# Two units of lead, second weights counted into it, and raw heads loaded in pairs: an attention and two MoEs on one core

## The chip, the core and the metric

One core of a Trainium2 chip runs one program: an attention of 4 batches, 8 heads, 576 positions and 64 dimensions a head, and two MoE layers over its 2304 tokens. The metric is the device time of one execution in microseconds (us); the median of three is 1420.57 (1418.37 to 1425.62). In this text PE is TensorE, DVE is VectorE, ACT is ScalarE, POOL is GpSimd and SP is SyncE, whose queue issues all transfers here.

## What is computed

The reference, cut to what matters (`B, H, S, D = 4, 8, 576, 64`):

```python
scores = (q @ k.T) / sqrt(D) + bias[h]          # bias[h][i, j]: a small MLP of log1p(|i - j|) / log1p(max(i, 1))
attn = exp(scores - max(scores)); attn /= sum(attn) + 1e-9
x = (attn @ v).transpose(0, 2, 1, 3).reshape(2304, 512)
g = x @ w_gate                                   # 512 x 1536
x = (g * sigmoid(g) * (x @ w_val)) @ w_out       # 1536 x 512
h = maximum(x @ w_in, 0)                         # 512 x 2048
out = (h * h) @ w_out2                           # 2048 x 512
```

The weights come as 64-bit floats, which are decoded on the chip. Each large product is made of three products of 16-bit halves.

## The kernel before, in words

**Work.** The attention is 144 *items*: ten phases (lines 52 and 938) of 4 or 8 heads, two batches a head. Phases 0 to 3, and the "m" among them, make batches 0 and 1, phases 5 to 9 batches 2 and 3. For an item, PE multiplies `qT` and `kT` (line 809), DVE adds the bias and finds the maximum (818), ACT takes the exponential (824), ACT or POOL casts it to 16 bits (833, 830), POOL makes the rest (222), SP issues the transpose of both halves into `pT` (852, three buffers of `pt` and of `pT`), and PE multiplies `pT` by the values (874). A phase over, `finish_unit` writes the normalised rows of one *unit* of 256 tokens to `x_d`, and `done[0]` says that MoE unit may start.

**First MoE.** Nine units (`moe1`, line 423): twelve steps of 24 matmuls (459), whose gate ACT and DVE make (`th`, lines 467 to 470), then POOL the low half of `z` (222), and 72 matmuls of `w_out` (481). A step's product stands in one of three PSUM banks. Around it run the decoding of the first weights (`w_stream`) and the bias (`bias_all`), whose matmuls are line 643.

**Second MoE.** `weights2` (line 1191) loads the second weights in 32 pieces of 512 KB into `w2s`, three rooms, decodes each on DVE (lines 258 to 263), scales them, and combines them in eight parts (`combine`, line 1164, on DVE, ACT and POOL). Then five chunks follow, each with a hidden part (1329) and an output part (1361).

**Order.** Python generators yield after each piece of work, and a loop at line 1275 takes the next step of the attention's side (`a_all`) or of the MoE's side (`m_all`). The MoE's side steps when `at[0]`, the items begun, has reached what `LEAD` gives for the work done so far in the MoE (`pos["m"]`; a unit counts 46.8):

```python
lead = w_done[0] >= 0 and at[0] >= float(np.interp(pos["m"], *LEAD))
if m_ok and (lead or not a_ok):
```

A scheduler then orders each engine's instructions; every engine, and SP's queue, takes its own in that order.

**Late heads.** Values and keys of batches 2 and 3 take the place of those of batches 0 and 1. Each head of one batch is loaded alone by `load_head` (line 675): a first part of 512 positions, and the last 64 positions twice, to both halves of the partitions, three transfers in all. `feed` (line 1072) calls it: values for their norm (`norm_v`) at items 32 to 47; keys from item 55 on, with `split_k` at items 56 to 71; values again at 58 to 73, with `split_v` an item later. The keys have two buffers (`late["k"]`), and so have the second values (`vr[:, 16]` and `late["v"]`, which lies in `wr`).

Of the kernel before, what the change touches and what calls it, by code (L numbers as in the profile page):

```python
# [10 lines left out]
F32 = mybir.dt.float32  # L11
F16 = mybir.dt.float16
# [9 lines left out]
B, H, S, D = 4, 8, 576, 64  # L22
DM, FF1, FF2 = 512, 1536, 2048
NT = B * S
P = 128
# [9 lines left out]
}  # L35

LEAD = [0, 47, 94, 140, 187, 234, 281], [16, 35, 53, 72, 97, 121, 144]
SQK = 16.0

CZ = 2.0 ** -48  # L40
# [36 lines left out]
def tile_attention_moe(  # L77
# [4 lines left out]
    nc = tc.nc  # L82
# [21 lines left out]
    st = {}  # L104
# [111 lines left out]
    def mixed(k):  # L216

        mix_n[k] = mix_n.get(k, -1) + 1
        return MIX[k][mix_n[k] % len(MIX[k])]
# [452 lines left out]
            nc.sync.dma_start(  # L672
                f[64 * e:64 * e + 64, :, 256:320], v[b, hs, 512:S, :].rearrange("h p d -> p h d"))

    def load_head(dst, src, n, b):

        nc.sync.dma_start(dst[:, 0:256], src[b, n, 0:512, :].rearrange("(p r) d -> p (r d)", r=4))
        for e in range(2):
            nc.sync.dma_start(dst[64 * e:64 * e + 64, 256:320], src[b, n, 512:S, :])

    def norm_v(bp, i, raw):
        nc.scalar.activation(junk1[:, 0:320], raw, AF.Square, accum_out=vss[bp][:, i:i + 1])
# [24 lines left out]
        st["sv", bp] = keep(16)  # L707
        nc.vector.tensor_copy(st["sv", bp], pb[:, 0:16])

    def split_v(bp, i, raw):  # L710

        o = vh[:, i, :].rearrange("p (c w) -> p c w", c=5)
        halves(o[:, :, 64:128], o[:, :, 0:64], raw.rearrange("p (c d) -> p c d", d=D),
               st["sv", bp][:, i:i + 1], mixed("V"))

    def split_k(i, raw):

# [295 lines left out]
    at = [0]  # L1013
# [30 lines left out]
    vr = att.tile([P, 17, 5 * D], F32, name="vr", bufs=1)  # L1044
# [16 lines left out]
    late = {}  # L1061

    def open_late():

        pre_stack.close()
        pool = a_stack.enter_context(tc.tile_pool(name="late", bufs=1, side="right"))
        lt = pool.tile([P, 960], F32, name="late")
        late["k"] = [lt[:, 320 * i:320 * i + 320] for i in range(2)]
        late["ks"] = lt[:, 640:960].bitcast(F16)
        late["v"] = wr.t[:, 36, 0:320]  # L1070

    def feed(idx, after):

        if not after:
            return
        if idx < 16:
            if idx in (1, 3):
                prep_k(2 + idx // 2)
            if 2 <= idx < 10:
                for i in (2 * idx - 4, 2 * idx - 3):  # L1080
                    norm_v(0, i, vr[:, i + 1, :])
            if idx == 12:
                scale_v(0, ma)
            if idx == 15:
                for j in range(6):
                    nc.gpsimd.memset(ptw[:, j // 2, 640 * (j % 2) + S:640 * (j % 2) + 640], 0.0)
        elif idx < 32:
            i = idx - 16
            split_v(0, i, vr[:, i + 1, :])
        elif idx < 48:  # L1090
            i = idx - 32
            if i:
                norm_v(1, i - 1, late["v"])
            load_head(late["v"], v, i // 2, 2 + i % 2)
        elif idx == 48:
            norm_v(1, 15, late["v"])
            scale_v(1, ma)

        i = idx - 56
        if -1 <= i < 15:  # L1100
            j = i + 1
            load_head(late["k"][j % 2], k, j // 2, 2 + j % 2)
        if 0 <= i < 16:
            split_k(i, late["k"][i % 2])
        if 2 <= i < 18:
            j = i - 2
            load_head((vr[:, 16, :], late["v"])[j % 2], v, j // 2, 2 + j % 2)
        if 3 <= i < 19:
            split_v(1, i - 3, (vr[:, 16, :], late["v"])[(i - 3) % 2])

    def start():
        load_k(0)
# [122 lines left out]
    def a_all():  # L1235
        yield from start()
        yield from merge((attend(), 25.5), (w_stream(), 70.0), (bias_all(), 29.0))
        yield from named(weights2(), "w")

    def m_all():  # L1240
        for m in range(9):
# [199 lines left out]
```

## Time and profile before

| what | value |
|---|---|
| median of three runs | 1420.57 us |
| the profiled execution | 1426.94 us |
| its span, first to last instruction | 1425.1 us |
| PE busy | 1159.7 us (81%) |
| DVE, ACT, POOL busy | 865.1, 662.5, 709.2 us |
| granted TensorE clock, mean | 0.904 |
| moved by DMA | 163.59 MB |

Busy is the time in which an engine worked on anything. An engine's share of the whole span says little here, since the stages have different limits: the first 199 us hold the first weights and the first phase, 199 to 830 the rest of the attention, and from 1140 on the chunks of the second MoE run alone. The granted clock is the share of full speed that the throttle let TensorE have.

### The profile page before, as it was taken

How to read it: one execution, taken by the hardware profiler on the slowest of the kernel's cores; microseconds unless marked ns; L12 is line 12 of the kernel's file. 1: busy time of each engine (PE TensorE's matmuls, PEld its weight loads, DVE VectorE, ACT ScalarE, POOL GpSimd, SP SyncE). 2: the span in 40 equal slices, each digit the busy share in tenths (PEclk: the TensorE clock that was granted, in tenths of full speed). 3: DMA queues.
4: the chain of work that ended last, by engine and by line, in shares of the span. 5: the costliest groups of instructions: out<-in, count | busy, mean ns of one | idle time of the engine just before them, and what ended most of it. 6: DMA issues, size and time to landing. Idle time of an engine off the chain costs nothing. (4 is left out here: it accounts for less than half of the span.)

```text
span 1425.1 us, 28069 instructions
## 1 busy us (share of the span) xinstructions
PE 1159.7 (81%) x10620; PEld 846.5 (59%) x10620; DVE 865.1 (61%) x1944; ACT 662.5 (46%) x1492; POOL 709.2 (50%) x766
## 2 busy tenths in 40 slices
PE   2459847988969943798998999958376899999998
PEld 2348736757648622575867676746133667667587
DVE  5997999854563543545446432248878666472925
ACT  5555676666654654445545532224452242332322
POOL 2763678667764522445555521103188844362713
PEclk9999868988978965699999999979687999999999
DMA  9776568577684667969899940065600102010000
GB/s 233 174 184 167 130 162 170 100 152 147 132 167 91 137 150 148 196 117 208 156 198 195 170 82 16 9 171 184 199 1 0 30 31 45 16 30 30 15 31 16
DMA packets 359507, 163.59 MB, mean 115 GB/s; under 512 B 323404, under 2 KB 334412, under 8 KB 359372
## 3 DMA queue, kind: packets, MB, share of 16 engines
q1 hardware_dynamic: 359372, 161.80, 51.5%
q8 instruction: 83, 1.36, 0.4%
q14 instruction: 52, 0.43, 0.1%
HBM read 76.94 MB, written 25.03 MB: 72 GB/s over the span
## 5 line engine op out<-in xcount | busy, mean ns | idle before, releaser
L459 PE MATMUL mm<-xT,wr 128*128 128x256 f16 x2592 | 310.4, 278 | 23.2 <-DMA xT<-x_d 15.4
L459 PEld LDWEIGHTS <-wr 128*128 128x128 f16 x2592 | 253.5, 100 | 61.1 <-issue 24.9
L1151 POOL TENSOR_TENSOR x<-x 128x256 f32<-128x256 f32 (+1 forms) x160 | 154.1, 972 | 150.2 <-ACT x L1338 145.2
L222 POOL TENSOR_TENSOR pt<-s,pt 128x576 f16<-128x576 f32 x128 | 167.2, 1311 | 91.9 <-ACT pt L833 81.5
L1329 PE MATMUL mm<-wr,w2r 128*128 128x512 f16 (+1 forms) x960 | 195.9, 366 | 0.0
L222 POOL TENSOR_TENSOR z<-th,z 128x256 f16<-128x256 f32 x108 | 78.8, 730 | 181.1 <-ACT z L442 171.6
L874 PE MATMUL av<-vr,pT 128*128 128x64 f16 (+3 forms) x2160 | 110.5, 208 | 54.3 <-DMA pT<-pt 41.1
L1329 PEld LDWEIGHTS <-w2r 128*128 128x128 f16 x960 | 95.5, 100 | 95.2 <-issue 8.5
L481 PE MATMUL mm<-wr,z 128*128 128x512 f16 x648 | 148.7, 379 | 0.0
L818 DVE CUSTOM_DVE_ANT_0 s<-qk,bh 128x576 f32<-128x576 f32 x144 | 107.8, 751 | 61.2 <-PE qk L809 32.0
L824 ACT ACTIVATE s<-s,sc 128x576 f32<-128x576 f32 x144 | 111.0, 771 | 67.8 <-DVE sc L823 51.5
L874 PEld LDWEIGHTS <-pT 128*128 128x128 f16 (+3 forms) x2160 | 90.0, 110 | 80.7 <-DMA pT<-pt 51.1
L618 POOL TENSOR_TENSOR btmp<-btmp,xs 128x256 f32<-128x256 f32 (+1 forms) x108 | 88.3, 820 | 97.6 <-ACT btmp L617 68.5
L1361 PEld LDWEIGHTS <-wr 128*128 128x128 f16 x1134 | 111.8, 99 | 31.5 <-DVE wr L1151 7.7
L809 PE MATMUL qk<-kT,qT 128*128 128x288 f16 x512 | 102.9, 339 | 16.6 <-DVE sc L818 9.9
L599 DVE TENSOR_TENSOR mask<-tabT,theta 128x1024 f16<-128x1024 f16 (+1 forms) x108 | 85.7, 809 | 34.2 <-PE ma L643 33.4
L468 DVE SCALAR_TENSOR_TENSOR th<-th,mm 128x256 f32<-128x256 f32 x108 | 45.0, 417 | 99.8 <-ACT th L467 99.6
L481 PEld LDWEIGHTS <-z 128*128 128x128 f16 x648 | 61.0, 98 | 67.0 <-issue 1.1
L1334 ACT ACTIVATE x<-mm 128x512 f32<-128x512 f32 (+1 forms) x80 | 43.6, 553 | 116.0 <-DVE wr L1151 57.0
L643 PEld LDWEIGHTS <-mask 128*128 128x128 f16 x1440 | 68.4, 113 | 46.5 <-DVE mask L599 23.4
L830 POOL TENSOR_SCALAR pt<-s 128x576 f16<-128x576 f32 x64 | 44.8, 700 | 86.4 <-ACT s L824 44.7
L624 POOL TENSOR_TENSOR bst<-bst,btmp 128x256 f32<-128x256 f32 (+1 forms) x108 | 83.6, 777 | 6.7 <-POOL btmp L618 0.5
(241 smaller groups left out, 2003.7 us busy)
## 6 DMA issues: line engine op xcount, KB each, us to landing
bh<-bias_d SPq DMA_DIRECT2D x64, 288.0 KB, 3.3
bias_d<-bst SPq DMA_DIRECT2D x36, 256.0 KB, 3.1
w2s<-in_moe_w_in_dram SPq DMA_DIRECT2D x16, 512.0 KB, 4.5
w2s<-in_moe_w_out_dram SPq DMA_DIRECT2D x16, 512.0 KB, 4.3
wr<-in_moe_w_gate_dram SPq DMA_DIRECT2D x24, 256.0 KB, 5.4
wr<-in_moe_w_val_dram SPq DMA_DIRECT2D x24, 256.0 KB, 4.7
wr<-in_moe_w_out_dram SPq DMA_DIRECT2D x9, 512.0 KB, 3.7
y_d<-yh SPq DMA_DIRECT2D x18, 256.0 KB, 2.6
```

Source lines behind the costliest of these rows:

```text
L222: nc.gpsimd.tensor_tensor(out=out_, in0=x, in1=hi, op=ALU.subtract)
L459: nc.tensor.matmul(pg[:, 256 * gi:256 * gi + 256], wr.parts(key, f // 4, cc, wl, P * (f % 4), P), mov(xl, cc), start=k == 0, stop=k == 11)
L481: nc.tensor.matmul(po, zall[:, f, zl, P * t:P * t + P], wr.parts("o", 0, f, wl), start=k == 0, stop=k == 3 * NF1 - 1)
L599: nc.vector.tensor_tensor(out=m[:, :, ni * e:ni * e + ni], in0=block(kb, i0, ni), in1=th, op=ALU.is_gt)
L618: nc.gpsimd.tensor_tensor(out=tmp[r], in0=tmp[r], in1=xb, op=ALU.mult)
L809: nc.tensor.matmul(pq[:, j, 0:288], qT[:, j0 + s, :], kT[:, 2 * n + i, js], start=s == 0, stop=s == 1)
L818: nc.vector.tensor_tensor_reduce(out=s.rearrange("p (a j) -> p a j", a=2), in0=pq[:, :, 0:288], in1=bias.rearrange("p (a j) -> p a j", a=2 ...
L824: nc.scalar.activation(s, s, AF.Exp, bias=nm, scale=-1.0, accum_out=total)
L874: nc.tensor.matmul(av[r, slot, 0:64], pT[:m, a, r], vh[:m, k0, o:o + 64], start=j == 0, stop=j == len(terms) - 1)
L1151: (nc.gpsimd if how else nc.vector).tensor_tensor(out=out_, in0=a, in1=b, op=op)
L1329: nc.tensor.matmul(ph[:, :n], w2r.parts("w", g // 4, cc, wl, P * (g % 4), P), yt[:, 4 * yl + cc, :], start=m == 0, stop=m == 11)
L1361: nc.tensor.matmul(po, HS[f][:, o:o + P], st["C7"][f][wl][:, b:b + 256], start=f == 0 and k == 0, stop=f == 7 and k == 2)
```

## The change

Three things change.

1. `LEAD` has new numbers. Unit 0 waits for item 32 (16 before), unit 1 for about 60, unit 2 for 88, unit 3 for 116, unit 4 for 144.
2. `at[0]` goes on to grow with the steps of `weights2`, which count 86.6 in all, so from unit 4 on the MoE's steps alternate with those of the second weights.
3. `load_head` gives way to `load_two`: a head of two batches at a time, one transfer for the first part and one for the tail, which goes to the lower 64 partitions only. It is called at every second item, and at the next both heads of the pair are normed or split. Keys and the first values share one buffer of two heads, `late["k"]`, whose upper half of the tail is cleared once by POOL; the second values have one pair in `late["v"]` and `late["vt"]`, and `split_v` makes two pieces of such a head, so ACT and DVE each have 16 instructions more, on 64 rows.

```diff
-LEAD = [0, 47, 94, 140, 187, 234, 281], [16, 35, 53, 72, 97, 121, 144]
+LEAD = [0, 47, 94, 141, 188, 330, 420], [32, 60, 88, 116, 144, 226, 232]
...
-    def load_head(dst, src, n, b):
-
-        nc.sync.dma_start(dst[:, 0:256], src[b, n, 0:512, :].rearrange("(p r) d -> p (r d)", r=4))
-        for e in range(2):
-            nc.sync.dma_start(dst[64 * e:64 * e + 64, 256:320], src[b, n, 512:S, :])
+    def load_two(main, tail, src, n, bp):
+
+        bs = slice(2 * bp, 2 * bp + 2)
+        nc.sync.dma_start(main, src[bs, n, 0:512, :].rearrange("b (p r) d -> p b (r d)", r=4))
+        nc.sync.dma_start(tail, src[bs, n, 512:S, :].rearrange("b p d -> p b d"))
...
-    def split_v(bp, i, raw):
+    def split_v(bp, i, raws_):
 
         o = vh[:, i, :].rearrange("p (c w) -> p c w", c=5)
-        halves(o[:, :, 64:128], o[:, :, 0:64], raw.rearrange("p (c d) -> p c d", d=D),
-               st["sv", bp][:, i:i + 1], mixed("V"))
+        c0 = 0
+        for raw in raws_:
+            m, n = raw.shape[0], raw.shape[1] // D
+            halves(o[:m, c0:c0 + n, 64:128], o[:m, c0:c0 + n, 0:64], raw.rearrange("p (c d) -> p c d", d=D),
+                   st["sv", bp][:m, i:i + 1], mixed("V"))
+            c0 += n
...
-        lt = pool.tile([P, 960], F32, name="late")
-        late["k"] = [lt[:, 320 * i:320 * i + 320] for i in range(2)]
-        late["ks"] = lt[:, 640:960].bitcast(F16)
-        late["v"] = wr.t[:, 36, 0:320]
+        lt = pool.tile([P, 1152], F32, name="late")
+        late["k"] = lt[:, 0:640].rearrange("p (b x) -> p b x", b=2)
+        nc.gpsimd.memset(late["k"][64:P, :, 256:320], 0.0)
+        late["ks"] = wr.t[:, 36, 0:320].bitcast(F16)
+        late["v"] = lt[:, 640:1152].rearrange("p (b x) -> p b x", b=2)
+        late["vt"] = wr.t[0:64, 36, 320:448].rearrange("p (b x) -> p b x", b=2)
...
         i = idx - 56
-        if -1 <= i < 15:
-            j = i + 1
-            load_head(late["k"][j % 2], k, j // 2, 2 + j % 2)
         if 0 <= i < 16:
-            split_k(i, late["k"][i % 2])
-        if 2 <= i < 18:
-            j = i - 2
-            load_head((vr[:, 16, :], late["v"])[j % 2], v, j // 2, 2 + j % 2)
+            if i % 2 == 0:
+                load_two(late["k"][:, :, 0:256], late["k"][0:64, :, 256:320], k, i // 2, 1)
+            else:
+                for j in range(2):
+                    split_k(i - 1 + j, late["k"][:, j, :])
         if 3 <= i < 19:
-            split_v(1, i - 3, (vr[:, 16, :], late["v"])[(i - 3) % 2])
+            if i % 2:
+                load_two(late["v"], late["vt"], v, (i - 3) // 2, 1)
+            else:
+                for j in range(2):
+                    split_v(1, i - 4 + j, [late["v"][:, j, :], late["vt"][:, j, :]])
...
-        yield from named(weights2(), "w")
+        for c in named(weights2(), "w"):
+            if not isinstance(c, tuple):
+                at[0] += c
+            yield c
```

The values for the norm, at items 32 to 47, change in the same way as the keys.

SP's queue while the late keys and values come in, before (`late` is a key buffer, `vr` and `wr` are value buffers, `pT` the transposed probabilities, `bh` a bias):

```order
L677 DMA late<-in_k_dram 128x256
L679 DMA late<-in_k_dram 64x64 x2
L677 DMA wr<-in_v_dram 128x256
L679 DMA wr<-in_v_dram 64x64 x2
L789 DMA bh<-bias_d_66 128x576
L852 DMA_TRANSPOSE pT<-pt 128x10x128
L677 DMA late<-in_k_dram 128x256
L679 DMA late<-in_k_dram 64x64 x2
L677 DMA vr<-in_v_dram 128x256
L679 DMA vr<-in_v_dram 64x64 x2
L852 DMA_TRANSPOSE pT<-pt 128x10x128
```

The same place now, where line numbers from 680 on are four higher (`late<-in_v_dram` is the first part of a pair of values, `wr<-in_v_dram` its tail):

```order
L856 DMA_TRANSPOSE pT<-pt 128x10x128 x2
L678 DMA late<-in_k_dram 128x2x256
L679 DMA late<-in_k_dram 64x2x64
L678 DMA late<-in_v_dram 128x2x256
L679 DMA wr<-in_v_dram 64x2x64
L793 DMA bh<-bias_d_66 128x576
L856 DMA_TRANSPOSE pT<-pt 128x10x128 x2
L678 DMA late<-in_v_dram 128x2x256
L679 DMA wr<-in_v_dram 64x2x64
L678 DMA late<-in_k_dram 128x2x256
L679 DMA late<-in_k_dram 64x2x64
```

Between two transposes stood the six transfers of one key head and one value head; now four transfers, of a pair of each, stand between two transposes and the next two.

DVE's queue where the decoding of the second weights begins, before (`xh` are the rows of unit 8, `w2r<-w2s` a decoding step, `th` the gate, here of unit 8, the last one):

```order
L921 SCALAR_TENSOR_TENSOR xh<-bh,ux,xh 128x256 x2
L921 SCALAR_TENSOR_TENSOR xh<-x_11859,ux,xh 128x256 x2
L258 TENSOR_SCALAR w2r<-w2s 128x512
L261 SCALAR_TENSOR_TENSOR w2r<-w2s,w2r 128x512
L263 SCALAR_TENSOR_TENSOR w2r<-w2s,w2r 128x512
L258 TENSOR_SCALAR w2r<-w2s 128x512
L261 SCALAR_TENSOR_TENSOR w2r<-w2s,w2r 128x512
L258 TENSOR_SCALAR w2r<-w2s 128x512
L263 SCALAR_TENSOR_TENSOR w2r<-w2s,w2r 128x512
L468 SCALAR_TENSOR_TENSOR th<-th,mm 128x256
L261 SCALAR_TENSOR_TENSOR w2r<-w2s,w2r 128x512
L470 SCALAR_TENSOR_TENSOR th<-th,mm 128x256
```

And now, where the gates are those of unit 4, with unit 5 behind it:

```order
L468 SCALAR_TENSOR_TENSOR th<-th,ma 128x256
L468 SCALAR_TENSOR_TENSOR th<-th,mm 128x256
L470 SCALAR_TENSOR_TENSOR th<-th,ma 128x256
L468 SCALAR_TENSOR_TENSOR th<-th,mm 128x256
L470 SCALAR_TENSOR_TENSOR th<-th,mm 128x256 x2
L258 TENSOR_SCALAR w2r<-w2s 128x512
L261 SCALAR_TENSOR_TENSOR w2r<-w2s,w2r 128x512
L263 SCALAR_TENSOR_TENSOR w2r<-w2s,w2r 128x512
L258 TENSOR_SCALAR w2r<-w2s 128x512
L468 SCALAR_TENSOR_TENSOR th<-th,ma 128x256
L261 SCALAR_TENSOR_TENSOR w2r<-w2s,w2r 128x512
L470 SCALAR_TENSOR_TENSOR th<-th,ma 128x256
```

The decoding stood after unit 7 and among the steps of unit 8; it now stands after the sixth step of unit 4 and among the steps of units 4 and 5, and most of the combination stands in units 6 and 7, the rest in unit 8, instead of after unit 8.

## Rows read from the trace of the kernel before

**Rows 1.** The page, part 1: engine, busy us (share of the span), instructions.

```profile
PE 1159.7 (81%) x10620; PEld 846.5 (59%) x10620; DVE 865.1 (61%) x1944; ACT 662.5 (46%) x1492; POOL 709.2 (50%) x766
```

**Rows 2.** Windows: stretch, length, busy us (instructions) of engines, granted clock, DMA.

```profile
199.00:494.00 295.00, 253.15 (x2932) 193.86 (x2931) 186.99 (x472) 179.89 (x445) 196.52 (x247) 0.87 0.68 138
494.00:588.00 94.00, 45.10 (x417) 29.91 (x415) 40.84 (x129) 45.23 (x94) 29.60 (x27) 0.59 0.74 159
588.00:830.00 242.00, 228.38 (x2430) 169.61 (x2429) 124.96 (x450) 127.05 (x289) 126.34 (x132) 0.97 0.92 174
635.00:670.00 35.00, 30.86 (x276) 18.64 (x275) 21.25 (x85) 21.46 (x48) 18.36 (x17) 0.91 1.02 203
830.00:930.00 100.00, 95.91 (x790) 69.98 (x787) 26.16 (x75) 27.40 (x65) 16.03 (x24) 1.00 0.10 23
930.00:1033.00 103.00, 57.84 (x439) 41.34 (x439) 77.57 (x199) 38.87 (x86) 18.33 (x19) 0.78 0.64 192
1033.00:1140.00 107.00, 83.29 (x444) 45.94 (x445) 83.22 (x93) 36.94 (x71) 90.22 (x78) 0.84 0.05 10
```

**Rows 3.** Windows of line 824 alone (exponential and its accumulator, two records an item).

```profile
494.00:588.00 94.00, 15.48 (x36) 0.59 0.74 159
635.00:670.00 35.00, 11.56 (x27) 0.91 1.02 203
```

**Rows 4.** Timeline of SP, 546 to 556: start us, us, engine, line, transfer, count.

```profile
546.11 1.33 SPq L852 DMA_TRANSPOSE pT<-pt  x1
547.48 0.70 SPq L677 DMA_DIRECT2D late<-in_k_dram  x1
548.58 1.13 SPq L679 DMA_DIRECT2D late<-in_k_dram  x2
549.76 0.58 SPq L677 DMA_DIRECT2D wr<-in_v_dram  x1
...
552.23 1.39 SPq L852 DMA_TRANSPOSE pT<-pt  x1
```

**Rows 5.** DMA issues, 494 to 588: transfer, count, KB each, median us to landing.

```profile
late<-in_k_dram SPq DMA_DIRECT2D x10, 128.0 KB, 2.7
vr<-in_v_dram SPq DMA_DIRECT2D x7, 128.0 KB, 2.2
wr<-in_v_dram SPq DMA_DIRECT2D x7, 128.0 KB, 2.4
...
late<-in_k_dram SPq DMA_DIRECT2D x20, 16.0 KB, 2.1
pT<-pt SPq DMA_TRANSPOSE x18, 3.8
```

**Rows 6.** Waits, 494 to 588: engine, line, for whom: us, times, longest.

```profile
POOL pt L222 <- ACT pt L833: 38.1, 8, 6.0
...
PE av L874 <- DMA pT<-pt: 26.0, 11, 4.2
```

**Rows 7.** DMA issues, 930 to 1033: the second weights.

```profile
w2s<-in_moe_w_in_dram SPq DMA_DIRECT2D x16, 512.0 KB, 4.5
w2s<-in_moe_w_out_dram SPq DMA_DIRECT2D x16, 512.0 KB, 4.3
```

**Rows 8.** Timeline of PE, unit 7 alone (columns as in rows 4).

```profile
881.74 1.25 PE L459 MATMUL mm<-xT,wr 128*128 128x256 f16 x10
883.52 28.98 PE L459 MATMUL mm<-xT,wr 128*128 128x256 f16 x264 [0.53 <-DVE yh L500]
912.34 15.70 PE L481 MATMUL mm<-wr,z 128*128 128x512 f16 x72
```

**Rows 9.** Timeline of PE, unit 8: its first and its last matmuls.

```profile
944.03 6.99 PE L459 MATMUL mm<-xT,wr 128*128 128x256 f16 x48 [11.38 <-DMA xT<-x_d]
...
997.60 8.58 PE L481 MATMUL mm<-wr,z 128*128 128x512 f16 x39
```

More of the change, by code (lines that the diff above doesn't have):

```diff
@@ L1088, in feed @@
             i = idx - 16
-            split_v(0, i, vr[:, i + 1, :])
+            split_v(0, i, [vr[:, i + 1, :]])
         elif idx < 48:
             i = idx - 32
-            if i:
-                norm_v(1, i - 1, late["v"])
-            load_head(late["v"], v, i // 2, 2 + i % 2)
+            if i % 2 == 0:
+                load_two(late["k"][:, :, 0:256], late["k"][0:64, :, 256:320], v, i // 2, 1)
+            else:
+                for j in range(2):
+                    norm_v(1, i - 1 + j, late["k"][:, j, :])
         elif idx == 48:
-            norm_v(1, 15, late["v"])
             scale_v(1, ma)
         i = idx - 56
-        if -1 <= i < 15:
-            j = i + 1
-            load_head(late["k"][j % 2], k, j // 2, 2 + j % 2)
         if 0 <= i < 16:
-            split_k(i, late["k"][i % 2])
-        if 2 <= i < 18:
-            j = i - 2
-            load_head((vr[:, 16, :], late["v"])[j % 2], v, j // 2, 2 + j % 2)
-        if 3 <= i < 19:
-            split_v(1, i - 3, (vr[:, 16, :], late["v"])[(i - 3) % 2])
+            if i % 2 == 0:
+                load_two(late["k"][:, :, 0:256], late["k"][0:64, :, 256:320], k, i // 2, 1)
+            else:
+                for j in range(2):
+                    split_k(i - 1 + j, late["k"][:, j, :])
+        if 3 <= i < 19:
+            if i % 2:
+                load_two(late["v"], late["vt"], v, (i - 3) // 2, 1)
+            else:
+                for j in range(2):
+                    split_v(1, i - 4 + j, [late["v"][:, j, :], late["vt"][:, j, :]])
     def start():
```

## The prediction

> **What bounds the kernel now.** I read the page first, then the span cut at the borders of the stages, then in each stage the waits and the queue that ends them. TensorE (PE) is busy 81% of the span [rows 1], so the question is where the other 19% lie and which of them the change can reach. Cut into stages [rows 2], PE is busy 253 of 295 us while items 16 to 61 of the attention run beside MoE units 0 to 2; 45 of 94 in the next stretch; 228 of 242 from 588 to 830, where the rest of the attention runs beside units 3, 4 and 5; 96 of 100 in units 6 and 7; and then 58 of 103 and 83 of 107 (at 0.84 of the clock) from 930 to 1140, where unit 8, the second weights and their combination stand. After 1140 PE is full.
>
> So there are two holes. The **first hole** is 494 to 588: 18 items (36 records of the exponential's line, two an item [rows 3]) in 94 us, 5.2 us each, with no MoE unit to fill PE. That isn't the attention's own pace: from 635 to 670 thirteen and a half items pass in 35 us, 2.6 us each [rows 3]. What differs is the raw keys and values of batches 2 and 3. SP's queue issues every transfer in order, and one cycle of it holds some 0.6 us for a head's first part, 1.1 for its two tails, the same again for a value head, and 1.3 to 1.4 for a transpose of probabilities [rows 4]. In the stretch it issues the first parts of 24 heads (10 + 7 + 7), their tails, two a head, 48, and 18 transposes [rows 5]; at 0.6, 0.56 and 1.36 us that is 14 + 27 + 25 = 66 us, and biases, queries and the transfers of finished units fill most of what is left. The waits agree: PE waits 26.0 us for transposed probabilities, and POOL 38.1 for a cast [rows 6] that needs a free probability buffer.
>
> The Trainium skill, "DMA: Bandwidth & Descriptors", section "Issuing engines are not separate DMA queues", says that the sequencer's time to start a transfer is "usually small relative to the DMA itself"; by that rule fewer issues would be worth next to nothing here, and the forecast would stand 28 us higher. The trace doesn't agree in this stretch: three issues of a head hold SP 1.7 us [rows 4] where its transfers land in 2.1 to 2.7 us, several in flight at once [rows 5].
>
> The **second hole** is 930 to 1140. The second weights come in 32 pieces [rows 7], all within 103 us; VectorE decodes them, then VectorE and POOL combine them, and PE has only unit 8 and the first hidden chunk meanwhile.
>
> **The change, part by part.** *The lead.* Today units 0 to 5 run inside the attention. Now units 0 to 3 do: unit 0 is let in at item 32 (16 before), unit 4 at 144, when the attention is over. A unit alone takes 1.2 + 29.0 + 15.7 = 46 us of PE [rows 8]. By item 62 two units have run in place of three, and from item 80 on two more in place of three.
>
> a. Items 16 to 61: 46 us of PE work leave a stretch where PE is 86% busy. Were PE the only limit the gain would be 46, were the items' own chain the limit, 0. I take 46 x 0.86 = 39, nearer to the first, since no other engine is as full there (POOL 197 and ACT 180 of 295 [rows 2]).
>
> b. The first hole. Twelve pairs in place of 24 heads: 72 issues become 24. A two-head issue isn't in the trace; from below it costs what a one-head issue does, 0.55 us, from above twice that, 1.2 us. SP saves 41 - 13 = 28 or 41 - 29 = 12 us. I take 0.6 us, so 27 us, since the nearest rows say so: a tail of 16 KB and a first part of 128 KB cost nearly the same [rows 4, 5]. As SP isn't quite full, that is some 28 us of time: 94 become 66, 3.7 us an item, still above the 2.6 of the quick stretch. Against it: one buffer now holds a pair, so the load of the next pair waits in SP's queue until this one is split, and transposes of probabilities are queued behind it, for which PE's weighted sums wait. In the new order two transposes and a pair of the other kind lie between two loads of one kind, 2 x 1.36 + 2 x 0.6 = 4 us, against 2.7 us to land [rows 5]: nearly covered. If that cover fails, the stretch keeps its 94 us (rival 2). A value head is now split in two pieces, which adds 16 ACT and 16 VectorE instructions on 64 rows beside engines that are half idle (ACT 45, VectorE 41 of 94 [rows 2]): nothing, or 5 us if all of them, some 0.3 us each, lay on the path. The same loads at items 32 to 47 spare SP a like amount while PE, not SP, is the fuller: nothing. The one new memset on POOL: nothing.
>
> c. Items 80 to 143: 46 us leave a stretch where PE is 94% busy. What takes over: 64 items at the quick 2.6 us are 168 us, and PE's remaining work is 228 - 46 = 182. Units 2 and 3 lie beside about 26 items each and fill PE there; a dozen items run alone. I take 3.2 us an item as the mean, 206 us in place of 242: 36 us. Ends: 0, if the items set today's pace, and 46.
>
> Together the attention ends 39 + 28 + 36 = 103 us sooner, at 727.
>
> d. Behind the attention. Today 310 us pass from 830 to 1140. In them stand three units, 138 us, and 83.3 x 0.84 = 70 us of the first chunk at full clock. Now there stand five units, 5 x 46 = 230, the same 70, and what the second weights still cost PE. Their loads, decoding and five of the eight combinations are counted into the lead and lie between units 4 to 7, the last three under unit 8, so the first chunk finds all ready. On VectorE a decoding step that waits for its load now stands ahead of the gate of units 4 and 5; behind it wait that step's th, POOL's part of z, and PE once its three banks are full. The 32 pieces need at most 103 us [rows 2, 7] and units 4 and 5 give 92: 11 us of stall. The combination costs PE today at most 107 - 70 = 37 us; five of its eight parts, 23 us, fall in units 6 and 7. Ends 0 and 23; I take 11. The attention's tail, which today lies in the 100 us of units 6 and 7 [rows 2] (92 of PE), is 8 us again. Sum 230 + 70 + 11 + 11 + 8 = 330 in place of 310; with 2 for the start of the first chunk, 22 us more.
>
> **Sum.** 1425.1 - 103 + 22 = 1344 us of span; with the 1.8 us that the profiled execution has around its span, 1346. That execution took 1426.9, and the median of the three runs, 1420.6, is 0.45% below it; the same share off gives **1340 us**.
>
> **Rivals.**
>
> 1. *Decoding holds the gate.* Beside sixteen decoded pieces a unit took from 944 to 1006, 62 us for 46 [rows 9]. If units 4 and 5 lose 16 each, 32 in place of 11, and the combination costs its full 23, that is 33 more: 1373 us. For it: VectorE takes its queue in order, and the decoding steps stand ahead of the gate's. Against it: sixteen pieces now lie beside more than one unit's steps. Chance 0.13.
>
> 2. *The single buffer eats the spared issues.* Then b is 0: 1368 us. It decides if a pair is split later than 4 us after its load was issued. For it: before, two buffers alternated and SP was still at its limit; against it, the landing of 2.7 us [rows 5]. The skill's rule on issue time, above, ends at the same time by another way. Chance 0.12.
>
> 3. *PE's clock falls.* In the first hole the granted clock was 0.59, most of it at the lower of the two levels, 1.2 GHz, after PE had stood half idle; in the full stretches it was 0.97 [rows 2]. More of the attention now runs without a unit. If units 2 and 3 ran at a granted 0.75 in place of 0.97, their 92 us would be 27 us longer: 1367. Against it: from 635 to 670 the clock was 0.91 although a unit filled only a part of it [rows 2]. Chance 0.06. The Trainium skill, "TensorE: Matmul & The Clock Gate", section "Part 1: The HAM clock gate", calls the throttled state the default which activity releases; that speaks against this change, and the trace agrees with it in the first hole.
>
> 4. *Slower: the round trip of the probabilities sets the pace of the whole attention.* If cast, transpose and landing through three buffers are what an item costs, with a unit beside it or without, and with few issues or many, then a, b and c are 0 and the 22 us behind remain: 1447 us of span, by the same steps 1442. It decides if items without a unit beside them don't go below 3.7 us. For it: PE's 26.0 us of waits in the hole [rows 6], and DMA engines at a share of 0.92 from 588 to 830 [rows 2]. Against it: 2.6 us an item from 635 to 670, at a DMA share of 1.02 [rows 2, 3]. Chance 0.08; and 0.05 that it holds for a part, c and half of a, and rival 2 with it, which ends within 0.5% of no change.
>
> **How the numbers follow.** The forecast keeps 0.56. Its own range is 1308 to 1370: from below a and c at 46 and 15 us less stall, from above a and c some 15 lower each. With rivals 1 to 3, and two of them together, the range reaches to 1400; rival 4 and gains beyond 1308 are left out. Less than 0.5%, 7 us, can't be told from no change. All but rival 4, whole or in part, end faster than that: faster 0.87, no change 0.05, slower 0.08.
>
> **What would show it.** Right: item 80 comes near 520 and item 143 near 725 us; the stretch of the key loads takes 60 to 70 us, with a third of the load issues; PE is over 90% busy from the end of the attention on, with no second hole. Wrong: SP waits for the splitting of late keys (rival 2), PE waits for th beside decoding (rival 1), a granted clock under 0.8 beside units 2 and 3 (rival 3), or items without a unit at 3.7 us or more outside the key loads (rival 4).

## The result and the profile after

The changed kernel takes **1370.53 us** in the median of four runs (1365.93 to 1375.43), beside 1420.89 for the kernel before on the same chip: ratio 0.9642, 95% interval 0.9596 to 0.9688, some 50 us. The forecast was 1340, the range 1308 to 1400. The profiled execution took 1365.93 us, its span is 1364.0, the mean granted clock 0.922. Between the two profiled executions lie 61 us, more than between the medians: this time the one before was above its median, and the one after below. Where a kernel's runs hold one far slower than the rest (bias_two_issues, one of 1578.44 us), its time and ratio leave that run out.

The page of the changed kernel, part 1 (before: [rows 1]); hardly any engine's work has changed, so most of the gain is idle time:

```profile
PE 1145.4 (84%) x10620; PEld 840.1 (62%) x10620; DVE 865.3 (63%) x1960; ACT 665.0 (49%) x1508; POOL 715.3 (52%) x767
```

To compare stretches of equal work I take the start of an item's exponential as a mark: item 16 (199 us before, 191 after), 62 (494, 459), 80 (588, 534) and 143 (827, 731). The windows of the changed kernel (columns as in [rows 2]): items 16 to 61, 62 to 79, the rest of the attention, then units 4, 5, 6, 7, 8, and the second MoE's chunks:

```profile
191.00:459.00 268.00, 207.99 (x2566) 157.75 (x2564) 178.18 (x430) 165.90 (x413) 188.02 (x234) 0.83 0.73 148
459.00:534.00 75.00, 50.85 (x517) 37.07 (x518) 46.47 (x160) 50.06 (x118) 32.05 (x30) 0.69 1.05 215
534.00:734.00 200.00, 175.76 (x1932) 129.88 (x1931) 109.34 (x396) 110.57 (x253) 116.81 (x119) 0.92 1.01 195
734.00:806.00 72.00, 59.02 (x540) 42.28 (x539) 44.73 (x118) 23.86 (x53) 11.76 (x15) 0.93 0.60 164
806.00:865.00 59.00, 54.10 (x423) 39.50 (x421) 52.13 (x130) 34.32 (x81) 18.84 (x20) 0.97 0.48 153
865.00:916.00 51.00, 47.05 (x344) 34.37 (x343) 27.70 (x75) 23.02 (x49) 38.92 (x39) 0.97 0.08 22
916.00:963.00 47.00, 47.00 (x363) 35.23 (x361) 13.81 (x39) 13.24 (x31) 10.80 (x15) 1.00 0.03 12
963.00:1009.00 46.00, 46.00 (x345) 33.50 (x343) 21.52 (x50) 14.10 (x33) 23.33 (x23) 1.00 0.14 36
1009.00:1364.00 355.00, 350.03 (x2464) 240.74 (x2462) 204.68 (x226) 112.56 (x206) 162.69 (x160) 1.00 0.10 25
```

Against [rows 2]: in items 16 to 61 PE has 45 us less to do (253 to 208), but the stretch is only 27 shorter. The first hole has shrunk from 94 to 75 us, and the DMA engines, at 0.74 before, are at 1.05. The rest of the attention has lost 42 us, and there too they are at 1.01. The second hole is gone: units 7 and 8 run with PE full, and so do the chunks. Units 4 and 5, where the second weights now come in, take 70 and 59 us from first gate to first gate (736, 806, 865), for 46 each alone.

The DMA issues in the first hole, 459 to 534 (before: [rows 5]), heads in pairs:

```profile
late<-in_v_dram SPq DMA_DIRECT2D x7, 256.0 KB, 3.3
late<-in_k_dram SPq DMA_DIRECT2D x5, 256.0 KB, 2.9
...
pT<-pt SPq DMA_TRANSPOSE x20, 4.4
wr<-in_v_dram SPq DMA_DIRECT2D x7, 32.0 KB, 2.5
late<-in_k_dram SPq DMA_DIRECT2D x5, 32.0 KB, 2.9
```

And SP's timeline inside it (before: [rows 4]; where a row has a count, its time reaches from the first start to the last end):

```profile
491.77 0.54 SPq L678 DMA_DIRECT2D late<-in_k_dram  x1
492.36 0.65 SPq L679 DMA_DIRECT2D late<-in_k_dram  x1
493.06 0.58 SPq L678 DMA_DIRECT2D late<-in_v_dram  x1
493.69 0.61 SPq L679 DMA_DIRECT2D wr<-in_v_dram  x1
494.34 0.59 SPq L793 DMA_DIRECT2D bh<-bias_d  x1
495.04 3.35 SPq L856 DMA_TRANSPOSE pT<-pt  x2
```

A pair costs SP about what one head did: term b's lower bound was near the truth. The 24 load issues sum to 15.0 us, 0.63 each, the 72 before to 41.4, 0.57 each: 26 us saved, 27 forecast. What SP issues in the whole stretch fell only from 83.0 of 94 to 66.2 of 75 us, since two more transposes and some biases and queries now fall in it; SP's filling is 0.88 both times.

### The profile page after: what moved, and what is told of

It reads as the page before. It is cut to its first block, busy times and chain, and to the rows that moved or that the text cites. A ratio compares the mean times of both kernels' runs of the same rounds, so it can differ in the third digit from the quotient of the medians.

```text
span 1364.0 us, 27913 instructions
## 1 busy us (share of the span) xinstructions
PE 1145.4 (84%) x10620; PEld 840.1 (62%) x10620; DVE 865.3 (63%) x1960; ACT 665.0 (49%) x1508; POOL 715.3 (52%) x767
## 3 DMA queue, kind: packets, MB, share of 16 engines
q8 instruction: 83, 1.36, 0.4%
## 4 chain that ended last, share of the span: by engine, by line
PE 49%; DMA 15%; DVE 14%; POOL 6%; issue 5%; ACT 4%; SPq 2%; POOLq 0%; ACTq 0%; DVEq 0%
PE mm L1341 14%; PE mm L1373 10%; DMA pT<-pt 9%; PE mm L459 9%; PE mm L481 5%; POOL pt L222 3%; DVE mask L599 3%; PE ma L459 2%; DMA w2s<-in_moe_w_in_dram 2%; PE ma L1373 2%; PE ma L481 2%; DVE s L822 2%; PE av L878 1%; DVE wr L193 1%; PE qk L813 1%
## 5 line engine op out<-in xcount | busy, mean ns | idle before, releaser
L459 PEld LDWEIGHTS <-wr 128*128 128x128 f16 x2592 | 259.6, 101 | 61.6 <-issue 20.3
L459 PE MATMUL mm<-xT,wr 128*128 128x256 f16 x2136 | 266.2, 283 | 12.6 <-DVE th L470 9.4
L1160 POOL TENSOR_TENSOR x<-x 128x256 f32<-128x256 f32 (+1 forms) x160 | 162.7, 1024 | 187.4 <-ACT x L1350 180.6
L1341 PE MATMUL mm<-wr,w2r 128*128 128x512 f16 (+1 forms) x960 | 187.5, 358 | 0.0
L878 PE MATMUL av<-vr,pT 128*128 128x64 f16 (+3 forms) x2160 | 104.5, 207 | 44.3 <-DMA pT<-pt 36.2
L878 PEld LDWEIGHTS <-pT 128*128 128x128 f16 (+3 forms) x2160 | 86.3, 109 | 66.9 <-DMA pT<-pt 43.9
L813 PE MATMUL qk<-kT,qT 128*128 128x288 f16 x512 | 99.6, 333 | 24.9 <-DVE sc L822 20.2
L1373 PEld LDWEIGHTS <-wr 128*128 128x128 f16 x1134 | 111.0, 98 | 13.7
L481 PE MATMUL mm<-wr,z 128*128 128x512 f16 x504 | 115.0, 382 | 0.0
L599 DVE TENSOR_TENSOR mask<-tabT,theta 128x1024 f16<-128x1024 f16 (+1 forms) x108 | 89.1, 840 | 23.4 <-PE ma L643 22.6
L1165 DVE CAST wr<-x 128x768 f16<-128x768 f32 (+3 forms) x60 | 60.4, 1007 | 38.0 <-ACT x L1350 25.5
```

Of the source, the lines that this page charges most:

```text
L459: nc.tensor.matmul(pg[:, 256 * gi:256 * gi + 256], wr.parts(key, f // 4, cc, wl, P * (f % 4), P), mov(xl, cc), start=k == 0, stop=k == 11)
L481: nc.tensor.matmul(po, zall[:, f, zl, P * t:P * t + P], wr.parts("o", 0, f, wl), start=k == 0, stop=k == 3 * NF1 - 1)
L599: nc.vector.tensor_tensor(out=m[:, :, ni * e:ni * e + ni], in0=block(kb, i0, ni), in1=th, op=ALU.is_gt)
L813: nc.tensor.matmul(pq[:, j, 0:288], qT[:, j0 + s, :], kT[:, 2 * n + i, js], start=s == 0, stop=s == 1)
L878: nc.tensor.matmul(av[r, slot, 0:64], pT[:m, a, r], vh[:m, k0, o:o + 64], start=j == 0, stop=j == len(terms) - 1)
L1160: (nc.gpsimd if how else nc.vector).tensor_tensor(out=out_, in0=a, in1=b, op=op)
```

## The experiments

The ratio is always to the kernel before, run beside it on the same chip. "Lead" is the new table, "counting" the growth of `at[0]` with the second weights, "pairs" the loads of two batches.

### The three parts

**lead_uncounted**: the kernel before with the new lead alone.

```diff
-LEAD = [0, 47, 94, 140, 187, 234, 281], [16, 35, 53, 72, 97, 121, 144]
+LEAD = [0, 47, 94, 141, 188], [32, 60, 88, 116, 144]
```

> The kernel before with the new lead for units 0 to 4 alone: heads are loaded one by one, and the steps of weights2 don't count, so units 4 to 8 follow the attention in one piece and the second weights stand beside unit 8 as before. Theory A (PE's work moved out of the attention comes back behind it, and only the counting pays for it): the attention ends some 75 us sooner, two more units (92 us) stand behind it, and the hole of 930 to 1140 stays: 1420 to 1440 us, no change or slower by up to 1.5%. Rival (the lead itself pays, since the attention's items run freer): under 1400 us.

Measured: 1456.9 us, ratio 1.0235 (1.0199 to 1.027).

**pairs_only**: the changed kernel with the old lead, uncounted.

```diff
-LEAD = [0, 47, 94, 141, 188, 330, 420], [32, 60, 88, 116, 144, 226, 232]
+LEAD = [0, 47, 94, 140, 187, 234, 281], [16, 35, 53, 72, 97, 121, 144]
...
-        for c in named(weights2(), "w"):
-            if not isinstance(c, tuple):
-                at[0] += c
-            yield c
+        yield from named(weights2(), "w")
```

> The kernel before with the raw heads in pairs alone, old lead. Theory A (SP's issues set the pace of the stretch of the key loads, and only there): 15 to 28 us less, 1393 to 1406 us, all of it between items 62 and 80, which take 66 to 79 us in place of 94. Rival (issues never mattered, or the single buffer gives them back): 1415 to 1425 us.

Measured: 1397.59 us, ratio 0.9811 (0.9785 to 0.9837).

**single_loads**: the kernel before with the new lead and the counting, heads loaded one by one.

```diff
-LEAD = [0, 47, 94, 140, 187, 234, 281], [16, 35, 53, 72, 97, 121, 144]
+LEAD = [0, 47, 94, 141, 188, 330, 420], [32, 60, 88, 116, 144, 226, 232]
...
-        yield from named(weights2(), "w")
+        for c in named(weights2(), "w"):
+            if not isinstance(c, tuple):
+                at[0] += c
+            yield c
```

> The changed kernel with the heads loaded one by one as before (new lead, weights2 counted). Theory A: it loses what the pairs gain, 15 to 28 us, and stands at 1385 to 1400 us. Rival (with the lead the stretch of the key loads is bound otherwise): within 7 us of the changed kernel's 1370.

Measured: 1399.66 us, ratio 0.9821 (0.9788 to 0.9854).

**pairs_lead_uncounted**: the changed kernel without the counting (the last lines of pairs_only's diff, and the lead of lead_uncounted).

> The changed kernel without the counting of weights2: the lead ends at unit 4, units 4 to 8 follow the attention in one piece and the second weights stand beside unit 8 and after it. Theory A: the attention ends at the changed kernel's 731 us, then 186 us for units 4 to 7, and the 103 + 107 us with unit 8, the second weights and the combination as before, and 285 us of chunks: 1405 to 1425 us. So the counting alone is worth 40 to 55 us and the lead pays only with it. Rival (the gain lies in the attention): under 1385 us.

Measured: 1432.37 us, ratio 1.0056 (1.0036 to 1.0077).

The stretches of all six, from the marks in each trace (us; "behind" is from item 143 to the end of the span):

| | items 16 to 62 | 62 to 80 | 80 to 143 | behind | ratio |
|---|---|---|---|---|---|
| before | 295 | 94 | 239 | 598 | 1 |
| lead_uncounted | 268 | 97 | 206 | 689 | 1.0235 |
| pairs_only | 295 | 69 | 243 | 598 | 0.9811 |
| single_loads (lead, counting) | 268 | 96 | 206 | 631 | 0.9821 |
| pairs_lead_uncounted | 268 | 76 | 198 | 693 | 1.0056 |
| after | 268 | 75 | 197 | 633 | 0.9642 |

The parts add up. Pairs are worth 0.0189 of the time alone (27 us), all of it in items 62 to 80, and 0.0179 beside lead and counting, of which the traces show 21 us there and 9 in items 80 to 143. Each of these kernels has an order of instructions of its own; but the pairs' gain in items 62 to 80 came three times (25, 21 and 21 us) and that of the counting twice, in kernels that differ in the rest. The lead alone loses 33 us: two units moved out of the attention shorten it by only 57 us (27 + 33, less 3) and cost 91 behind it. What pays is the counting, 58 to 60 us, all of it behind the attention: it lays the second weights under the units that the lead has put there. Both kernels with the lead and without the counting came out above their expected ranges, by 17 and 7 us: in lead_uncounted the attention became 57 us shorter where 75 were expected, in pairs_lead_uncounted 693 us lie behind it where 681 were. Without the counting the second hole stands, only later; lead_uncounted, windows:

```profile
965.00:1015.00 50.00, 32.27 (x288) 27.23 (x288) 35.00 (x81) 17.08 (x35) 10.12 (x11) 0.87 0.73 206
1015.00:1065.00 50.00, 23.31 (x150) 13.05 (x148) 41.18 (x104) 22.23 (x51) 10.08 (x10) 0.74 0.59 179
1065.00:1115.00 50.00, 35.37 (x154) 16.20 (x155) 40.61 (x55) 23.72 (x46) 43.08 (x38) 0.81 0.00 0
```

For 150 us PE is busy 91, while DVE decodes and combines, as in [rows 2] from 930 to 1140. The first hole without pairs, single_loads:

```profile
466.00:562.00 96.00, 52.94 (x520) 37.36 (x520) 46.16 (x142) 49.21 (x106) 34.66 (x33) 0.68 0.73 156
```

Nearly the same PE work as after (50.85), the same lead, but 96 us and DMA engines at 0.73 instead of 75 and 1.05: the engines could have carried the bytes, and SP's issues, 84.9 of 96 us, held them back.

### What sets the pace of items 80 to 143

Here SP issues in 0.82 of the time, the DMA engines are at 1.01, PE is busy 176 of 200. Four kernels act on the bias loads, which are 288 KB each.

**bias_two_issues**: each load in two halves. **bias_copied_too**: each also copied to a place in DRAM that nothing reads.

```diff
-        nc.sync.dma_start(bt, bias_d[PHASES[ph][0]][:, n, :])
+        for j in range(2):
+            nc.sync.dma_start(
+                bt[:, 288 * j:288 * j + 288], bias_d[PHASES[ph][0]][:, n, 288 * j:288 * j + 288])
```

```diff
+    extra = dram.tile([P, 80, S], F32, name="extra")
...
+        nc.sync.dma_start(extra[:, 8 * ph + n, :], bias_d[PHASES[ph][0]][:, n, :])
```

> The changed kernel with each head's bias loaded in two halves: 72 issues of SP more, some 0.55 us each, 40 us of SP's time, and no byte more. Theory S (SP's issues still set the pace of the attention): the attention ends 20 to 35 us later, ratio to before 0.978 to 0.990. Theory E (the DMA engines, at a share of 1.0 from 534 to 734, set it now): 0 to 12 us later, ratio 0.964 to 0.973.

> The changed kernel with a second issue for each head that copies its bias, 288 KB, to a place in DRAM that nobody reads: the same 72 issues more as in bias_two_issues, and 20 MB more for the DMA engines. Theory E: 30 us or more above bias_two_issues. Theory S: within 10 us of bias_two_issues.

Measured: 1386.2 us, ratio 0.9726 (0.9682 to 0.9769), and 1390.1, ratio 0.975 (0.9696 to 0.9805); items 80 to 143 took 215 and 219 us. By their expectations both speak for SP's issues. For bias_copied_too the trace forbids that reading: of its 72 copies, which wait for no buffer, only 8 were issued behind 548 us, the last at 596. The trace's row of 64 of them (line, queue, operation; ns of the issue, least, median and most; first and last start in us):

```profile
L795 SPq DMA_DIRECT2D extra<-bias_d x64: 469/537/1130, 91.2 to 596.1; - x64
```

Eight issues of 0.5 us don't make 22 us. In bias_two_issues SP's issues in the stretch did grow, from 164.5 to 183.0 us, and the stretch by 18. But in both kernels the scheduler has ordered all engines' instructions anew: of DVE's 393 in this stretch only 266 and 257 follow one another as in the changed kernel. Both runs are inconclusive.

**bias_on_act**: the loads issued from ACT's queue.

```diff
-        nc.sync.dma_start(bt, bias_d[PHASES[ph][0]][:, n, :])
+        nc.scalar.dma_start(bt, bias_d[PHASES[ph][0]][:, n, :])
```

> The changed kernel with each head's bias load issued from ACT's queue instead of SP's: 64 of the issues of the items after 16, some 0.6 us each, leave SP; bytes and everything else stay. Theory S (SP's issue time sets a part of the pace of the items): what bias_two_issues showed with its sign turned, a third to a half of some 36 us, so items 80 to 143 take about 185 us instead of 197 and the whole 12 to 18 us less: ratio to the kernel before 0.952 to 0.957. Theory E (the DMA engines set it, they carry the same bytes): no change, ratio 0.962 to 0.967. Third way: a load that waits in ACT's queue for a free bias buffer holds the exponentials behind it, and the items get slower: ratio above 0.970.

Measured: 1383.51 us, ratio 0.9713 (0.9675 to 0.9751). SP's issues fall from 164.5 to 151.1 us, and the stretch takes 201 us (197 after): the 12 us that Theory S expected didn't come. The whole is some 10 us slower, 7 of it in items 16 to 62. That is the third way's number without its mechanism, for before none of the bias loads did ACT's queue wait longer than 1.05 us. The window, with the DMA engines' share still at 1.00:

```profile
538.00:738.00 200.00, 171.74 (x1928) 127.02 (x1927) 111.15 (x397) 109.24 (x250) 115.89 (x116) 0.93 1.00 195
```

**bias_eighth**: from phase 5 on only three bias loads are whole; the others bring 72 of 576 columns, so a part of the bias is left out.

```diff
+    kept, turns = [], [0]
...
-        hold["bias", ph, n] = bt = att.tile([P, S], F32, tag="bh", name="bh", bufs=3)
-        nc.sync.dma_start(bt, bias_d[PHASES[ph][0]][:, n, :])
+        w = S if ph < 5 or len(kept) < 3 else 72
+        if w == S:
+            bt = att.tile([P, S], F32, tag="bh", name="bh", bufs=3)
+            if ph >= 5:
+                kept.append(bt)
+        else:
+            bt = kept[turns[0] % 3]
+            turns[0] += 1
+        hold["bias", ph, n] = bt
+        nc.sync.dma_start(bt[:, 0:w], bias_d[PHASES[ph][0]][:, n, 0:w])
...
-                xr = att.tile([P, S], F32, tag="bh", name="bh", bufs=3)
+                xr = late["x"] if kept else att.tile([P, S], F32, tag="bh", name="bh", bufs=3)
...
+        late["x"] = lt[:, 0:S]
```

> The changed kernel, but from phase 5 on (items 72 to 143) only the first three bias loads are whole; the 33 after them keep their issue on SP's queue, their buffers and their waits, and load 72 of 576 columns (the rest of the buffer keeps an earlier head's bias, so that part of the computation is left out). Theory E, after bias_on_act stated anew: from item 80 on the 16 DMA engines are full (share 1.01 over 200 us), a whole bias holds them 128 x 138 ns / 16 = 1.1 us, and SP's issues only fill the gaps. Then some 28 loads less 0.9 us each leave 25 us: items 80 to 143 take 172 to 180 us instead of 197 (PE's 176 busy us there are the next bound), the whole 17 to 25 us less, ratio to the kernel before 0.946 to 0.953. Theory S (SP's issue time sets the pace): SP issues the same transfers, 195 to 199 us, ratio 0.962 to 0.967.

Measured: 1369.36 us, ratio 0.9633 (0.9573 to 0.9693), no change; items 80 to 143 take 196 us:

```profile
542.00:739.00 197.00, 173.89 (x1923) 128.25 (x1920) 111.75 (x394) 109.95 (x251) 115.23 (x117) 0.94 0.91 157
```

The share of the DMA engines fell from 1.01 to 0.91, SP's issues from 164.5 to 153.8 us, and nothing became faster. So neither theory is borne out. Neither is refuted, either: in this stretch bias_on_act and bias_eighth are ordered anew like the first two (276 and 269 of DVE's 393 instructions in the old order), and a new order alone can cost such times. xd_on_act (below), which leaves the bias loads alone and keeps 315 in order, takes 206 us here.

The changed kernel's own trace says more, if it is cut at its units: unit 2 runs until 609, unit 3 from 630 to 716.

```profile
534.00:609.00 75.00, 67.89 (x697) 49.73 (x696) 41.24 (x140) 40.64 (x94) 42.37 (x44) 0.98 1.00 193
609.00:630.00 21.00, 14.29 (x173) 10.03 (x171) 12.63 (x59) 14.06 (x33) 13.21 (x13) 0.81 1.12 203
630.00:716.00 86.00, 80.60 (x853) 59.97 (x851) 46.15 (x157) 45.21 (x103) 50.16 (x52) 0.97 1.00 198
```

From 609 to 630, with no unit beside them, items pass at 2.5 us each, with the DMA engines at 1.12 and SP issuing in 0.90 of the time. Beside a unit an item takes 3.2 us, with the DMA engines at 1.00, SP at 0.82 and PE busy 148 of 161 us. There neither SP nor the DMA engines do the most that they do in this kernel, and PE is nearest to full. What makes up the 24 us in which PE is idle between 534 and 734, 15.9 of them waits for transposed probabilities, stays open.

### Behind the attention

**unit4_free** and **unit4_free_slow**: the second weights begin a unit later, and in the second they are also spread over a longer part.

```diff
-LEAD = [0, 47, 94, 141, 188, 330, 420], [32, 60, 88, 116, 144, 226, 232]
+LEAD = [0, 47, 94, 141, 188, 235, 330, 420], [32, 60, 88, 116, 144, 144, 226, 232]
```

```diff
-LEAD = [0, 47, 94, 141, 188, 330, 420], [32, 60, 88, 116, 144, 226, 232]
+LEAD = [0, 47, 94, 141, 188, 235, 376, 420], [32, 60, 88, 116, 144, 144, 226, 232]
```

> The changed kernel with one more point in the lead: unit 4 isn't held back by the steps of weights2 (a flat stretch from 188 to 235 at 144), which then alternate with units 5 and 6, and the combination falls in unit 7. Theory A (unit 4 took 72 us and unit 5 59 us for 46 because the finishing of unit 8 and the first decoding steps stand ahead of their gates on VectorE): unit 4 takes about 51 us as without the counting, units 5 to 7 share what the decoding and combination cost, 10 to 20 us less in all, ratio to before 0.950 to 0.957. Rival (the attention's tail starves PE whatever stands behind, or the loss only moves one unit on): ratio 0.962 to 0.970.

> As unit4_free, but the steps of weights2 are spread over three units (235 to 376) instead of two. Theory A with the pieces' transfer as the limit of the decoding: spread wider, decoding waits less ahead of the gates: 0 to 6 us better than unit4_free. Rival (the order is the scheduler's, which expects shorter transfers, and the combination comes too late for unit 8): equal or up to 8 us worse.

Measured: 1372.78 us, ratio 0.9613 (0.9567 to 0.9659), and **1360.88 us, ratio 0.9556 (0.951 to 0.9602)**, the fastest of all kernels run, 0.9% below the changed one (the two intervals still overlap by 0.0006; from item 143 on the traces lie 7 us apart). Units from first gate to first gate (unit 8 to its last product):

| | unit 4 | 5 | 6 | 7 | 8 | sum |
|---|---|---|---|---|---|---|
| after | 70 | 59 | 51 | 47 | 44 | 271 |
| unit4_free | 51 | 60 | 58 | 56 | 44 | 269 |
| unit4_free_slow | 51 | 59 | 58 | 52 | 44 | 264 |

Unit 4 is freed in both, as Theory A said. But in unit4_free the five units together gain 2 us and not 10 to 20: units 6 and 7 lose most of what unit 4 gains, as the rival said. Spread wider, the weights cost 5 us less. The weights cost a unit that they lie beside some 13 us wherever that is; beyond this, unit 4 of the changed kernel has a stall of its own. Its DVE timeline (a bracket is idle time and what ended it):

```profile
742.06 0.42 DVE L468 SCALAR_TENSOR_TENSOR th<-th,mm 128x256 f32<-128x256 f32 x1 [0.52 <-ACT th L467]
742.52 0.42 DVE L470 SCALAR_TENSOR_TENSOR th<-th,mm 128x256 f32<-128x256 f32 x1
750.12 0.49 DVE L902 TENSOR_TENSOR x<-av,sc 128x128 f32<-128x128 f32 x2 [7.18 <-PE av L878]
...
757.96 0.88 DVE L925 SCALAR_TENSOR_TENSOR xh<-x,ux,xh 128x256 f16<-128x256 f32 x2 [2.44 <-ACT xh L924]
759.66 0.42 DVE L468 SCALAR_TENSOR_TENSOR th<-th,ma 128x256 f32<-128x256 f32 x1 [0.81 <-ACT th L467]
```

Between two gates of unit 4 (lines 468, 470) lie 17 us in which DVE's queue holds the attention's last rows (902 to 925, unit 8's): it waits 7.2 us for PE's last weighted sum, and POOL's part of `z` waits 17.2 in its turn. Steps of the same rows stand in the queues of ACT and PE. In unit4_free_slow unit 4's next gates come every 3 us at the same place:

```profile
744.23 0.42 DVE L470 SCALAR_TENSOR_TENSOR th<-th,mm 128x256 f32<-128x256 f32 x1
747.27 0.42 DVE L468 SCALAR_TENSOR_TENSOR th<-th,mm 128x256 f32<-128x256 f32 x1 [2.62 <-ACT th L467]
747.73 0.42 DVE L470 SCALAR_TENSOR_TENSOR th<-th,mm 128x256 f32<-128x256 f32 x1
749.89 0.42 DVE L468 SCALAR_TENSOR_TENSOR th<-th,mm 128x256 f32<-128x256 f32 x1 [1.74 <-ACT th L467]
```

Then come the weights. The waits of the changed kernel, 734 to 806 (as in [rows 6]):

```profile
POOL z L222 <- ACT z L442: 42.5, 9, 17.2
...
DVE w2r L258 <- DMA w2s<-in_moe_w_in_dram: 10.2, 9, 3.1
```

**xd_on_act**: the stores of finished rows, which stand ahead of the last transpose on SP, moved to ACT's queue.

```diff
-            nc.sync.dma_start(x_d[u][P * i:P * i + P, :], xh.rearrange("p l e -> p (l e)"))
+            nc.scalar.dma_start(x_d[u][P * i:P * i + P, :], xh.rearrange("p l e -> p (l e)"))
```

> The changed kernel with the stores of finished rows (x_d, a transfer for each part of a unit) issued from ACT's queue instead of SP's. At the end of the attention these stores, which wait for DVE's rows, stand in SP's queue ahead of the last transposes and of the first load of a second weight, which was issued only 22 us after unit 4 began. If that order costs unit 4 a part of its 26 us, unit 4 takes up to 7 us less and the whole 3 to 7 us less, ratio 0.959 to 0.962; if unit 4 waits for the attention's own last rows on DVE, nothing changes: 0.963 to 0.967.

Measured: 1376.04 us, ratio 0.9669 (0.964 to 0.9699): no gain. Unit 4 takes 70 us again, and the stall is there as before, five us later:

```profile
755.04 0.49 DVE L902 TENSOR_TENSOR x<-av,sc 128x128 f32<-128x128 f32 x2 [7.17 <-PE av L878]
```

So the place of the stores in SP's queue doesn't cause it. What fits the traces is the place of those rows in the queues of DVE, ACT and PE, ahead of the gates of two steps of unit 4 whose products PE had ended by 749.0; in unit4_free_slow, where the gates stand first, the stall is gone.

**free_slow_bias_act**: unit4_free_slow with bias_on_act's line.

> The lead of unit4_free_slow together with the bias loads on ACT's queue. If the two lie in different stretches (units 4 to 8 behind the attention, items 16 to 143 inside it), their gains add: 9 us of the one and 12 to 18 us of the other off the changed kernel, ratio to the kernel before 0.945 to 0.951. If the bias loads gain nothing, 0.955 to 0.960 as unit4_free_slow.

Measured: 1374.65 us, ratio 0.9649 (0.9616 to 0.9682). The gains don't add: 13 us slower than unit4_free_slow alone, so here too the kernel with the bias loads on ACT's queue, in its own order, is the slower one.

## Why the prediction was right, and where it was off

Direction and mechanism held: the first hole was shortened and the second closed in the way that was forecast. The size was too large, 80 us against 50. The measured 1370.53 stands at the upper edge of the forecast's own range (1308 to 1370); it is inside 1400 by the room left for rivals, none of which came whole. Term by term, profile to profile:

| term | forecast | measured |
|---|---|---|
| a, items 16 to 61 | -39 | 295 to 268: -27 |
| b, the first hole | -28 | 94 to 75: -19 |
| c, items 80 to 143 | -36 | 239 to 197: -42 |
| d, behind the attention | +22 | 598 to 633: +35 |
| sum from item 16 on | -81 | -53 |
| up to item 16 | 0 | 199 to 191: -8 |

**a was mis-sized by its factor.** PE lost the 45 us of work that the step gave, but its idle time rose from 42 to 60 us. I took the share in which PE was busy, 0.86, as the share of removed work that comes back as time; 27 of 46 came back, 0.59. The four kernels with the new lead in the table of the parts all take the same 268 us, so this belongs to the lead alone. An average over 295 us hid the reason. Of the 18 us more of idle time 12 lie ahead of unit 0's first product, where DVE, which my list of full engines left out, is busy 97% of the time. Before, this lasts from 199 to 239, after, with unit 0 held back, from 191 to 259:

```profile
199.00:239.00 40.00, 26.16 (x318) 19.94 (x317) 38.91 (x80) 27.75 (x65) 34.09 (x32) 0.65 0.82 169
191.00:259.00 68.00, 42.46 (x513) 33.21 (x512) 66.12 (x130) 46.25 (x101) 54.62 (x52) 0.58 0.84 155
```

Nor is it the items' own chain that holds the end of the stretch: from item 55 to item 56 (394 to 445, before 418 to 479) none begins, and DVE's wait ends at 443.6 with the load of the next bias, whose store had landed at 440.6.

**b had SP's saving right and the rest wrong.** 26 us of issues went, and pairs_only, with nothing else changed, brings 94 to 69 us. Beside the new lead it is 75: SP's queue still fills 0.88 of a stretch into which two more transposes have moved; the 20 of them take 31.0 us of issue, 1.55 each, where I had used 1.36. Rival 2 has fallen: SP waited 2 us in all for the splitting of a pair. By the rule of the Trainium skill, "DMA: Bandwidth & Descriptors", "Issuing engines are not separate DMA queues", that starting a transfer usually takes little beside the transfer itself, b would have been next to nothing. The runs disagree for this stretch: 96 issues fewer in the whole kernel gave 25 to 27 us. In the next stretch they don't decide it: bias_on_act took issues off SP and nothing became faster, but in another order.

**c was nearly right**, with 3.1 us an item in place of 3.2, and 176 us of PE's remaining work in place of 182. Part of it belongs to the pairs: without them the stretch takes 206 us. Two of its products are slips (64 x 2.6 is 166 and not 168, 64 x 3.2 is 205 and not 206); they move the term by 1 us.

**d was mis-sized in decoding and tail.** Units 4 to 7 lost 24, 13, 5 and 1 us, 43 in all, where 30 stood. The combination cost some 6 us (units 6 and 7) where 11 stood, and unit 8 and the chunks were clean. The attention's tail cost some 14 where 8 stood: the stall of unit 4 behind the attention's last rows, which I had not seen, since I let the tail cost PE's work alone and didn't ask what stands behind it on DVE. That leaves 23 for the decoding beside units 4 and 5 where 11 stood. These 11 rested on a misread row: 103 us is the length of a window. The 32 loads were issued within 83 us before and 87 after, less than the 92 of two units, so by that sum the stall would have been nothing. DVE waited 12 us for pieces all the same, 10.2 of them in unit 4. Nor are the 14 us simply to be had back: without the stall, unit4_free is 2 us shorter over the five units. Of rival 1, decoding that holds the gate, the first half came near (32 us for units 4 and 5; 37 measured, with the stall), the second didn't (23 for the combination; 6 measured).

**Rival 3** has not happened: beside units 2 and 3 the granted clock was 0.98 and 0.97. In the first hole it rose from 0.59 to 0.69, with PE busy 0.68 of the time instead of 0.48. **Rival 4** has fallen: from 609 to 630, without a unit and behind the key loads, an item took 2.5 us, not 3.7.

**The last step, to the median, was no error of its own.** It took 6 us off because the profiled execution before lay above its median, which is the same as taking the 81 us from the median. The terms were 28 us too large from item 16 on, and 8 us came up to item 16 that no term had. Such 8 us are within chance: in ten of these kernels the work up to there is the same, and the mark lies anywhere from 191 to 200 us.

## What to carry to other kernels

Moving work out of a crowded stretch pays there only by the part of the time in which that work's engine ends the waits, not by its busy share over a long stretch, so cut the stretch where the work begins and ends; and it costs its full length where it goes. It is worth doing if it covers another hole, and the move and the cover must be made together (the lead alone lost 33 us, the counting gave 60). Where a queue's issue time fills a stretch, count issues rather than bytes; but a resource that reads full, as SP at 0.82 or the DMA engines at 1.01, isn't shown to be the limit until a run that takes from it becomes faster. Where a scheduler orders the instructions, compare that order first: a run that moved a third of them tests the new order as well. When work is put behind the end of another chain, read what that chain's last instructions hold up in the queue of every engine they share.

## What the runs showed of the hardware

- The issue time on SP didn't grow with the transfer: in the first hole the median was 0.54 us for the 256 KB of a pair of keys, 0.62 for those of values, and 0.62 for the 32 KB of their tails; for the 512 KB pieces of the second weights it was 0.33.
- A share of the 16 DMA engines of 1.01 wasn't the most they did: it was 1.05 in the first hole and 1.12 from 609 to 630 of the same execution. The 256-byte packets, most of them the transposes', held an engine 22 ns each at a share of 0.74 and 23 at 1.05 (first hole, before and after); they make 159 of the 202 us of engine time from 534 to 734.
- Two kernels with their 288 KB loads on ACT's queue instead of SP's were 10 and 13 us slower. No run here separates the queue from the new order that the scheduler made.
